# Second MoE: 104 columns for a slot's last chunk, and a stretch without choices behind slot 2

## The chip, the cores and the metric

The kernel runs on one core of a Trainium2 chip. The metric is the device time of one execution in microseconds (us). The kernel before took 532.64 us (median of three runs, 532.51 to 535.22).

## The reference, cut to what matters

Attention over two batches of 448 tokens feeds a first gated MoE layer (`a * b @ w_out`), and its 896 rows of 768 numbers feed the second MoE, which the change is about:

```python
def _moe2_ref(x, expert_emb, tau, w1, w2):        # x 896x768, 8 experts, w1 768x1024, w2 1024x768
    ...
    expert_idx = np.argmax(logits, axis=1)        # one expert a token
    ...
    for e in range(E):
        mask = expert_idx == e
        if not mask.any():
            continue
        h = np.maximum(x[mask] @ w1[e], 0.0)
        out[mask] = gate_w[mask, None] * (h @ w2[e])
```

How many tokens an expert gets is known only on the chip. On the inputs of these runs the counts are, in falling order, 329, 227, 203, 77, 44, 16, 0 and 0 (the reference's own choice of experts gives them).

## The kernel before, in words

**Stages.** Attention and the first MoE take until 367 us. Beside the first MoE's last product (L897), `choose`, `places` and `tables` route the tokens: they count them, sort the experts by their counts into eight *slots*, the largest first, and write a table of row numbers for each slot. `places` also writes one number `many` (L797 to L800: the larger of slot 3's count less 64 and slot 4's count), which `count_many` puts into a register of every engine; `counts` does that with each slot's count.

**A slot and its chunks.** A slot's tokens are taken in chunks of 128 (called windows, `w`). One chunk is this work:
- `gather` (POOL) fetches the token rows by an indirect DMA, `turn2` (PE, L1081) transposes them, and ACT copies them to `xt`.
- `first` (L1088) makes the hidden rows: 144 products on PE (L1099 to L1101). The weights of the expert are the stationary operand (128 columns loaded), and the chunk's `n` tokens are the columns that move. ACT writes the relu twice (L1107, L1108), POOL the low half (L1109).
- `second` (L1135): 48 products (L1151), the hidden rows of the tokens stationary, 256 or 512 columns of the second weights moving; ACT scales the result (L1155), and POOL scatters it to the output (`scatter`, L1115).

`whole(j)` is a slot's first chunk, always of 128 columns, and `more(j, w)` are its others: behind a condition `cv[j] > w * P` (L1192) stand the chunk and, nested in it, the condition for the next one. From slot 4 on, a slot with at most 64 tokens goes through `part` instead, with 64 columns (`first` with n = 64, `second_small` L1128). For slot 4 `many` decides between the two (the condition labelled `s4`, L1261): where it is at most 64, `chain` runs the rest as parts, each behind a condition on its count (`c4_5`, L1255).

**Choices.** A condition is a compare and branch that each engine which takes part in it executes in its own order of instructions. `more`'s conditions are taken by PE, ACT and POOL; those of `s4`, the chain and the late slots also by DVE and SP. `hint` and `hint_slot` (L1173, L1179) tell the engines of a condition's outcome ahead of it. At the end of a nested condition each engine runs a wait for its own outstanding work before it goes on.

**The weights.** SP issues the loads of an expert (L864, L866; 14 pieces) into four raw buffers, DVE splits each piece into a high and a low half (L877, L881) in one of three buffers, `bufA`, `bufB`, `bufC` in turn. `load_expert(j + 2)` stands ahead of slot j's work; from expert 5 on it is behind a condition of its own on DVE and SP (L1168). So expert 5 is loaded while slots 2, 3 and 4 run, into the buffer that slot 2 uses.

**The order now.** With the counts above PE runs slot 0 with three chunks, slots 1 and 2 with two each, slot 3 with one, all of 128 columns; then slots 4 and 5 as parts of 64. The order of instructions in this stage is that of the code; the first MoE's planner has no part in it.

Of the kernel before, what the change touches and what calls it, by code (L numbers as in the profile page):

```python
# [12 lines left out]
F32 = mybir.dt.float32  # L13
I32 = mybir.dt.int32
# [3 lines left out]
ALU = mybir.AluOpType  # L18
# [67 lines left out]
def fused_kernel(ctx: ExitStack, tc: tile.TileContext, q, k, v, w_a, w_b, w_out, emb, tau, w1, w2, out):  # L86
    nc = tc.nc
    B, NPR, _, S = q.shape
# [12 lines left out]
    SQ = -1.0 / math.sqrt(D)  # L101

    NLOAD, FEW = 5, 4
    NFIRST, NC1 = 4, 8
    RK = dict(S=(-2.0, 5.0, -1.0), M=-1.2, T=-8.1, H=-6.8, L=0.0, V=2.7, sq=5.4, X=-9.5, C1A=10, C1B=13.0)
    NRAW2 = 4
# [660 lines left out]
    def places():  # L767
# [25 lines left out]
        nc.vector.tensor_reduce(meta[:, 1, :], tmp, axis=AX.X, op=ALU.add)  # L793
        metai = cst.tile([1, 2, E], I32, name="metai")
        nc.vector.tensor_copy(metai, meta[0:1])
        mny = cst.tile([1, 1], F32, name="mny")
        nc.vector.scalar_tensor_tensor(mny, meta[0:1, 1, FEW - 1 : FEW], -P / 2.0, meta[0:1, 1, FEW : FEW + 1], op0=ALU.add, op1=ALU.max)  # L797
        nc.vector.tensor_scalar(mny, mny, 0.0, None, op0=ALU.max)
        mnyi = cst.tile([1, 1], I32, name="mnyi")
        nc.vector.tensor_copy(mnyi, mny)  # L800
        R["many"] = mnyi

# [174 lines left out]
            skip_runtime_bounds_check_because="only compared with constants")[1]  # L977

    def count_many():
        cv["many"] = nc.values_load_multi_w_load_instructions(  # L980
            R["many"], engines=ALL, min_val=0, max_val=NT,
            skip_runtime_bounds_check_because="only compared with a constant")[1][0]

    for j in range(0, E, 2):
        at(G2(3, 2 + 2 * j), 9, lambda j=j: counts(j))
# [81 lines left out]
    def gather(j, w):  # L1067
        io = bass.IndirectOffsetOnAxis(ap=gidi[:, j * NW + w : j * NW + w + 1], axis=0)
        nc.gpsimd.indirect_dma_start(xr_(j, w), None, xs, io)  # L1069

    def turn2(j, w):
        xt = xt_(j, w)
        xr = xr_(j, w).bitcast(F16)
        if w == 0:
            pt = ps.tile([P, 2048], F16, tag="big1", name=f"ptx{j}_{w}", bufs=1)
            halves = [pt[:, :DM], pt[:, DM : 2 * DM]]
        else:
            halves = [ps.tile([P, 1024], F16, tag=g, name=f"ptx{j}_{w}{g}", bufs=1)[:, :DM] for g in ("sm", "held")]
        for l, pt_ in enumerate(halves):
            for kc in range(KC):  # L1080
                nc.tensor.transpose(pt_[:, kc * P : (kc + 1) * P], xr[:, (l * KC + kc) * P : (l * KC + kc + 1) * P], id16)  # L1081
        if w == 0:
            nc.scalar.activation(xt.rearrange("p k t -> p (k t)"), pt[:, : 2 * DM], AF.Copy)
        else:
            for l in range(2):
                nc.scalar.activation(xt[:, l * KC : (l + 1) * KC, :].rearrange("p k t -> p (k t)"), halves[l], AF.Copy)
# [48 lines left out]
    def second(j, w, n, mid=()):  # L1135
        u = f"{j}_{w}_{n}"
        hth, htl = hs[min(w, 1)]
        _, _, w2h, w2l = expert(j)
        py = big(f"py{u}", min(w, 1))
        parts = (slice(512, DM), slice(0, 512))  # L1140
        halves = (range(FC // 2), range(FC // 2, FC))
        for k, (a, fs, p) in enumerate([(hth, fs, p) for fs in halves for p in range(2)] + [(htl, range(FC), p) for p in range(2)]):
            if k == 3:
                for fn in mid:
                    fn()
                if w == 0 and j + 1 > FEW:
                    hint_slot(j + 1)
            ns = parts[p]
            for f in fs:
                for w_ in (w2h, w2l) if a is hth else (w2h,):  # L1150
                    nc.tensor.matmul(py[:, ns], a[:, f, :], w_[:, f, ns], start=k < 2 and f == 0 and w_ is w2h,  # L1151
                                     stop=a is htl and f == FC - 1)
        y = m2y.tile([P, DM], F32, tag="y", name=f"y{u}", bufs=1)
        for ns in parts:
            nc.scalar.activation(y[:n, ns], py[:n, ns], AF.Copy, scale=scl[:n, j * NW + w : j * NW + w + 1])  # L1155
        scatter(j, w, n, y)
# [13 lines left out]

    def hint(j, w):
        if w < nwin[j]:
            tc.mark_branch_hint_location(f"w{j}_{w}", hint=cv[j] > w * P, engines=EN)  # L1173

    def hint_slot(j):
        if NLOAD <= j < E:
            tc.mark_branch_hint_location(f"w{j}_0", hint=cv[j] > 0, engines=ALL)
        elif j == FEW:
            tc.mark_branch_hint_location(f"s{j}", hint=cv["many"] > P // 2, engines=ALL)  # L1179

    def ahead(j, w):

        return j < NEXT1 if w == 1 else j < 2 and w == 2

    def next_turns(j, w):
        return [lambda: turn2(j, w + 1)] if w + 1 < nwin[j] and ahead(j, w + 1) else []

    def more(j, w):

        if w == nwin[j]:  # L1190
            return
        with tc.If(cv[j] > w * P, preferred_fallthrough_block=True, label=f"w{j}_{w}"):  # L1192
            hint(j, w + 1)
            if not ahead(j, w):
                gather(j, w)
                turn2(j, w)
            first(j, w, P)
            second(j, w, P, next_turns(j, w))
            more(j, w + 1)

    NEXT1 = 3

# [11 lines left out]
        nc.scalar.activation(raw[:1, :1], xt_(0, 1)[:1, 0, :1], AF.Copy)  # L1214
        return raw

    def whole(j):
        mid = next_turns(j, 0)
        if j == 0:
            first(0, 0, P, lambda: (hint(0, 1), gather(0, 1), gather(1, 0)))  # L1220
            gather(0, 2)
            gates()
            windows()
            scaled()
            mid += [lambda: load_expert(2, True)]
        else:
            if j >= FEW:
                hint(j, 1)
            if j + 1 == FEW:
                hint_slot(FEW)  # L1230
            first(j, 0, P, lambda: hint(j, 1) if j + 1 < FEW else None)
            gathers(j)
        if j >= FEW:
            more(j, 1)
        if j + 1 < E:
            mid += [lambda: turn2(j + 1, 0)]
        if j == 0:
            mid += [scales, lambda: gathers(0)]
        second(j, 0, P, mid)
        if j + 1 < FEW:  # L1240
            more(j, 1)

    def part(j):
# [14 lines left out]
                chain(i, j + 1)  # L1258

    def slot(j):  # L1260
        with tc.If(cv["many" if j == FEW else j] > P // 2, preferred_fallthrough_block=True, label=f"s{j}") as many:  # L1261
            if j == FEW:
                more(j - 1, 1)
                load_expert(j + 2)
            whole(j)
            slots(j + 1)
        with many.Else():
            if j == FEW:
                load_expert(j + 2)
            chain(j, j)  # L1270

    def slots(j):
        if j == E:
            return
        if j < FEW:
            if 0 < j < E - 2:
                load_expert(j + 2)
            whole(j)
            slots(j + 1)
        elif j < NLOAD:  # L1280
            slot(j)
        else:
            with tc.If(cv[j] > 0, preferred_fallthrough_block=True, label=f"w{j}_0"):
                if j < E - 2:
                    load_expert(j + 2)
                slot(j)
# [43 lines left out]
```

## Time and profile before

| | |
|---|---|
| median of three runs | 532.64 us |
| the profiled execution | 532.47 us, of which the span of its instructions is 530.8 us |
| PE busy in the span | 508.7 us, 96% |
| DVE, ACT, POOL busy | 402.9, 212.0, 118.6 us |
| second MoE's chunks (from the end of L897 to PE's last product) | 367.2 to about 524 us |
| from there to the end of the span | 7 us |

An execution's own time is a little longer than the span of its instructions (1.7 us here). In the rows below, times are microseconds from the start of the span. PE is TensorE's matmul part, PEld its loads of the stationary operand, PEq (PEldq) its sequencer, where branches and waits run; DVE, ACT, POOL and SP are the other engines. In a row of the timeline the first number is the start, the second the duration, the brackets the idle time of that engine just before with what ended it. A matmul's duration reaches from its start to the end of its results, so that the durations of neighbours overlap: how long one takes in a row of many is read from start to start.

### The profile page before, as it was taken

What the parts mean: (1) busy time and instruction counts of PE and PEld (TensorE: products, weight loads), DVE (VectorE), ACT (ScalarE), POOL (GpSimd) and SP (SyncE); (2) the same over time, 40 slices, a digit from 0 to 9 for tenths busy, and PEclk for the clock granted to TensorE, in tenths of its full rate; (3) what the DMA queues carried; (4) which work ended last, traced back from release to release, by engine and by line L of the source; (5) the groups of instructions that cost most, each with busy time, mean ns of one, the idle gap of its engine ahead of it and who ended that gap; (6) DMA issues with size and microseconds to landing.
All of it is one profiled execution on the core that took longest, in us unless ns stands there. A gap on an engine that the chain in (4) does not pass through costs nothing. (4 is left out here: it accounts for less than half of the span.)

```text
span 530.8 us, 12641 instructions
## 1 busy us (share of the span) xinstructions
PE 508.7 (96%) x5121; PEld 343.4 (65%) x5121; DVE 402.9 (76%) x643; ACT 212.0 (40%) x492; POOL 118.6 (22%) x123
## 2 busy tenths in 40 slices
PE   6999799999999999999999999999999999999994
PEld 3777477765555555545547666667788778876883
DVE  3899589999999966899712579984589497694970
ACT  3888998896233222343310111113422133231232
POOL 7877445110000000000000000000532242233333
PEclk9999799999999999999999999999999999999998
DMA  7853313036356533789720189991597479584761
GB/s 221 280 165 92 127 53 114 7 116 127 130 192 207 190 111 119 198 195 268 190 40 3 61 308 291 315 315 50 153 325 250 136 229 325 181 250 181 217 201 48
DMA packets 44793, 92.63 MB, mean 175 GB/s; under 512 B 22118, under 2 KB 25190, under 8 KB 44720
## 3 DMA queue, kind: packets, MB, share of 16 engines
q1 hardware_dynamic: 42816, 83.77, 50.7%
q0 software_dynamic: 1904, 7.90, 4.8%
q8 instruction: 45, 0.74, 0.6%
q14 instruction: 28, 0.23, 0.1%
HBM read 79.46 MB, written 8.26 MB: 165 GB/s over the span
## 5 line engine op out<-in xcount | busy, mean ns | idle before, releaser
L502 PE MATMUL ab<-bufA 128*128 128x448 f16 x864 | 167.7, 352 | 0.0
L502 PEld LDWEIGHTS <-bufA 128*128 128x128 f16 x864 | 83.3, 98 | 74.7
L897 PE MATMUL x<-woc,gL 128*128 128x512 f16 x336 | 56.5, 326 | 0.0
L392 ACT ACTIVATE pr<-sc,mn 112x336 f32<-112x336 f32 (+2 forms) x96 | 46.6, 499 | 12.3 <-DVE mn L376 12.3
L1003 POOL DMA_INDIRECT x<-xse,gidi x1 | 1.3, 1277 | 222.7 <-DMA rw<-in_moe_w_dram 222.7
L897 PEld LDWEIGHTS <-gL 128*128 128x128 f16 x336 | 32.4, 98 | 21.0
L376 DVE TENSOR_REDUCE mn<-sc 112x2 f32<-112x896 f32 (+3 forms) x48 | 33.9, 726 | 8.4 <-PE sc L365 8.2
L1109 POOL TENSOR_TENSOR hl<-hr,hh 128x512 f16<-128x512 f32 (+1 forms) x20 | 26.4, 1320 | 61.0 <-ACT hr L1108 56.2
L359 PE MATMUL sc<-ld,ld 64*112 64x448 f32 (+3 forms) x192 | 35.7, 473 | 4.0 <-DMA ld<-in_q_dram 4.0
L407 DVE TENSOR_TENSOR tbuf<-pt,tbuf 112x448 f16<-112x448 f32 x60 | 35.9, 612 | 4.3 <-ACT tbuf L404 4.0
L401 PE MATMUL pt<-id,pr 112*112 112x112 f32 x240 | 34.8, 272 | 4.1 <-ACT pr L392 2.6
L260 DVE SCALAR_TENSOR_TENSOR cv<-raw,cv 128x768 uint32<-128x768 uint32 x36 | 34.4, 955 | 0.9
L404 ACT ACTIVATE tbuf<-pt 112x448 f16<-112x448 f32 x60 | 32.6, 550 | 5.9 <-PE pt L401 5.6
L264 DVE SCALAR_TENSOR_TENSOR cv<-raw,cv 128x768 uint32<-128x768 uint32 x36 | 34.4, 954 | 0.4
L881 DVE SCALAR_TENSOR_TENSOR bufC<-rw,bufC 128x768 f16<-128x768 f32 (+1 forms) x28 | 33.2, 1185 | 1.4
L1151 PEld LDWEIGHTS <-hh 128*128 128x128 f16 x256 | 24.4, 98 | 14.6
L510 DVE TENSOR_TENSOR asb<-asb,ab 128x448 f32<-128x448 f32 x24 | 14.8, 618 | 24.7 <-PE ab L502 24.5
L1107 ACT ACTIVATE hh<-ph 128x512 f16<-128x512 f32 (+1 forms) x20 | 11.1, 554 | 54.4 <-PE ph L1101 54.4
L881 DVE SCALAR_TENSOR_TENSOR bufA<-rw,bufA 128x768 f16<-128x768 f32 (+1 forms) x28 | 30.0, 1073 | 1.4
L881 DVE SCALAR_TENSOR_TENSOR bufB<-rw,bufB 128x768 f16<-128x768 f32 (+1 forms) x28 | 30.0, 1072 | 1.4
L903 ACT ACTIVATE row<-x 128x768 f16<-128x768 f32 x7 | 5.7, 810 | 63.3 <-PE x L897 54.4
L877 DVE TENSOR_SCALAR bufC<-rw 128x768 f16<-128x768 f32 (+1 forms) x28 | 19.3, 688 | 13.4 <-PEq L1192 7.4
(243 smaller groups left out, 1199.4 us busy)
## 6 DMA issues: line engine op xcount, KB each, us to landing
rw<-in_moe_w_dram SPq DMA_DIRECT2D x36, 512.0 KB, 4.8
rw<-in_moe_w_dram SPq DMA_DIRECT2D x48, 384.0 KB, 3.9
raw<-in_moe_w_a_dram SPq DMA_DIRECT2D x12, 768.0 KB, 6.0
raw<-in_moe_w_b_dram SPq DMA_DIRECT2D x12, 768.0 KB, 7.6
raw<-in_moe_w_out_dram SPq DMA_DIRECT2D x12, 768.0 KB, 4.3
ld<-in_k_dram SPq DMA_DIRECT2D x12, 224.0 KB, 4.6
ld<-in_q_dram SPq DMA_DIRECT2D x12, 224.0 KB, 2.7
ld<-in_v_dram SPq DMA_DIRECT2D x12, 224.0 KB, 4.5
```

The source lines that it names most:

```text
L260: nc.vector.scalar_tensor_tensor(t, r()[:, :, 1], 0xC0000000, t, op0=ALU.bitwise_and, op1=ALU.bitwise_or)
L264: nc.vector.scalar_tensor_tensor(t, r()[:, :, 0], 29, t, op0=ALU.logical_shift_right, op1=ALU.bitwise_or)
L359: nc.tensor.matmul(sc[:CP, j, o : o + W], qt[hd, c * CP : W], kt[hd, :W], start=n == 0, stop=False)
L376: nc.vector.tensor_reduce(mns[pi][:, c, :], sc[:CP, :, o : o + W], axis=AX.X, op=ALU.min)
L392: nc.scalar.activation(pr[:, d : d + W], sc[:CP, jj, o : o + W], AF.Exp, bias=mn[:, c, jj : jj + 1], scale=-1.0, accum_out=sums[pi][:, c, ...
L401: nc.tensor.transpose(pt[:CP, cs], prs[g][:, cs], id32[:CP, :CP])
L404: nc.scalar.activation(tbufs[g % NTB][:, 0, :S], pts[g][:CP, :S], AF.Copy)
L407: nc.vector.tensor_tensor(tbufs[g % NTB][:, 1, :S], pts.pop(g)[:CP, :S], tbufs[g % NTB][:, 0, :S], op=ALU.subtract)
L502: nc.tensor.matmul(gt[i][:, :S], w[:, h, i, kc, :], x[:, kc, ts], start=kc == n == 0, stop=kc == KC - 1 and n == 2)
L881: nc.vector.scalar_tensor_tensor(dl, R.pop(("raw", j, pc))[:, :n], SE, dh, op0=ALU.mult, op1=ALU.subtract)
L897: nc.tensor.matmul(xp[:, ns], G(f)[:, a, tk], woc[:, f, l, ns], start=st, stop=sp)
L1109: nc.gpsimd.tensor_tensor(lv, hr, hv, op=ALU.subtract)
```

## The change

- A new constant TAIL = 104. A chunk after the first with more than 104 tokens runs with 128 columns as before (`chunk(j, w, P)`); the condition of `more` is now `cv[j] > w * P + TAIL`. It has an else branch, `tail(j, w)`: behind a condition of its own without a label or a hint stands the same chunk with 104 columns.
- In `second` the stationary operand and the output are cut to the chunk's n tokens, `a[:, f, :n]` and `py[:n]`.
- `places` writes two numbers, `s` (the old `many`) and `light`: the largest of slot 3's count less 40, slot 4's count, and slot 2's count less 168.
- Behind slot 2's first chunk stands a new condition `light`, taken by all five engines, with its hint in slot 2's `whole`. Where `light` is over 64, the code goes on as before. Else: slot 2's tail, the load of expert 5 (under its own condition), slot 3 with 104 columns, the load of expert 6 (likewise), then the chain of parts from slot 4. Slot 3's condition for a second chunk and the condition `s4` don't stand on that way.

With the counts of these inputs `light` is max(77 - 40, 44, 203 - 168) = 44, so the else way is taken. The tails are slot 0's third chunk (329 - 256 = 73 tokens, at most 104), slot 1's second (99) and slot 2's second (75); slot 3 (77) is whole with 104 columns.

```diff
--- before.py
+++ after.py
@@ -101,6 +101,7 @@
     SQ = -1.0 / math.sqrt(D)
 
     NLOAD, FEW = 5, 4
+    TAIL = 104
     NFIRST, NC1 = 4, 8
     RK = dict(S=(-2.0, 5.0, -1.0), M=-1.2, T=-8.1, H=-6.8, L=0.0, V=2.7, sq=5.4, X=-9.5, C1A=10, C1B=13.0)
     NRAW2 = 4
@@ -793,10 +794,13 @@
         nc.vector.tensor_reduce(meta[:, 1, :], tmp, axis=AX.X, op=ALU.add)
         metai = cst.tile([1, 2, E], I32, name="metai")
         nc.vector.tensor_copy(metai, meta[0:1])
-        mny = cst.tile([1, 1], F32, name="mny")
-        nc.vector.scalar_tensor_tensor(mny, meta[0:1, 1, FEW - 1 : FEW], -P / 2.0, meta[0:1, 1, FEW : FEW + 1], op0=ALU.add, op1=ALU.max)
-        nc.vector.tensor_scalar(mny, mny, 0.0, None, op0=ALU.max)
-        mnyi = cst.tile([1, 1], I32, name="mnyi")
+        mny = cst.tile([1, 2], F32, name="mny")
+        at_ = lambda j: meta[0:1, 1, j : j + 1]
+        nc.vector.tensor_scalar(mny[:, :1], at_(FEW - 1), -P / 2.0, 0.0, op0=ALU.add, op1=ALU.max)
+        nc.vector.tensor_scalar(mny[:, 1:], at_(FEW - 1), float(P // 2 - TAIL), 0.0, op0=ALU.add, op1=ALU.max)
+        nc.vector.tensor_tensor(mny, mny, at_(FEW).to_broadcast([1, 2]), op=ALU.max)
+        nc.vector.scalar_tensor_tensor(mny[:, 1:], at_(FEW - 2), float(P // 2 - P - TAIL), mny[:, 1:], op0=ALU.add, op1=ALU.max)
+        mnyi = cst.tile([1, 2], I32, name="mnyi")
         nc.vector.tensor_copy(mnyi, mny)
         R["many"] = mnyi
 
@@ -977,9 +981,9 @@
             skip_runtime_bounds_check_because="only compared with constants")[1]
 
     def count_many():
-        cv["many"] = nc.values_load_multi_w_load_instructions(
+        cv["s"], cv["light"] = nc.values_load_multi_w_load_instructions(
             R["many"], engines=ALL, min_val=0, max_val=NT,
-            skip_runtime_bounds_check_because="only compared with a constant")[1][0]
+            skip_runtime_bounds_check_because="only compared with a constant")[1]
 
     for j in range(0, E, 2):
         at(G2(3, 2 + 2 * j), 9, lambda j=j: counts(j))
@@ -1148,7 +1152,7 @@
             ns = parts[p]
             for f in fs:
                 for w_ in (w2h, w2l) if a is hth else (w2h,):
-                    nc.tensor.matmul(py[:, ns], a[:, f, :], w_[:, f, ns], start=k < 2 and f == 0 and w_ is w2h,
+                    nc.tensor.matmul(py[:n, ns], a[:, f, :n], w_[:, f, ns], start=k < 2 and f == 0 and w_ is w2h,
                                      stop=a is htl and f == FC - 1)
         y = m2y.tile([P, DM], F32, tag="y", name=f"y{u}", bufs=1)
         for ns in parts:
@@ -1170,13 +1174,13 @@
 
     def hint(j, w):
         if w < nwin[j]:
-            tc.mark_branch_hint_location(f"w{j}_{w}", hint=cv[j] > w * P, engines=EN)
+            tc.mark_branch_hint_location(f"w{j}_{w}", hint=cv[j] > w * P + TAIL, engines=EN)
 
     def hint_slot(j):
         if NLOAD <= j < E:
             tc.mark_branch_hint_location(f"w{j}_0", hint=cv[j] > 0, engines=ALL)
         elif j == FEW:
-            tc.mark_branch_hint_location(f"s{j}", hint=cv["many"] > P // 2, engines=ALL)
+            tc.mark_branch_hint_location(f"s{j}", hint=cv["s"] > P // 2, engines=ALL)
 
     def ahead(j, w):
 
@@ -1189,14 +1193,23 @@
 
         if w == nwin[j]:
             return
-        with tc.If(cv[j] > w * P, preferred_fallthrough_block=True, label=f"w{j}_{w}"):
+        with tc.If(cv[j] > w * P + TAIL, preferred_fallthrough_block=True, label=f"w{j}_{w}") as full:
             hint(j, w + 1)
-            if not ahead(j, w):
-                gather(j, w)
-                turn2(j, w)
-            first(j, w, P)
-            second(j, w, P, next_turns(j, w))
+            chunk(j, w, P, next_turns(j, w))
             more(j, w + 1)
+        with full.Else():
+            tail(j, w)
+
+    def chunk(j, w, n, mid=()):
+        if not ahead(j, w):
+            gather(j, w)
+            turn2(j, w)
+        first(j, w, n)
+        second(j, w, n, mid)
+
+    def tail(j, w):
+        with tc.If(cv[j] > w * P, preferred_fallthrough_block=True):
+            chunk(j, w, TAIL)
 
     NEXT1 = 3
 
@@ -1214,7 +1227,7 @@
         nc.scalar.activation(raw[:1, :1], xt_(0, 1)[:1, 0, :1], AF.Copy)
         return raw
 
-    def whole(j):
+    def whole(j, n=P):
         mid = next_turns(j, 0)
         if j == 0:
             first(0, 0, P, lambda: (hint(0, 1), gather(0, 1), gather(1, 0)))
@@ -1226,9 +1239,11 @@
         else:
             if j >= FEW:
                 hint(j, 1)
-            if j + 1 == FEW:
+            elif j == FEW - 1 and n == P:
                 hint_slot(FEW)
-            first(j, 0, P, lambda: hint(j, 1) if j + 1 < FEW else None)
+            elif j == FEW - 2:
+                tc.mark_branch_hint_location("light", hint=cv["light"] > P // 2, engines=ALL)
+            first(j, 0, n, lambda: hint(j, 1) if j < FEW - 2 else None)
             gathers(j)
         if j >= FEW:
             more(j, 1)
@@ -1236,8 +1251,8 @@
             mid += [lambda: turn2(j + 1, 0)]
         if j == 0:
             mid += [scales, lambda: gathers(0)]
-        second(j, 0, P, mid)
-        if j + 1 < FEW:
+        second(j, 0, n, mid)
+        if j < FEW - 2:
             more(j, 1)
 
     def part(j):
@@ -1258,7 +1273,7 @@
                 chain(i, j + 1)
 
     def slot(j):
-        with tc.If(cv["many" if j == FEW else j] > P // 2, preferred_fallthrough_block=True, label=f"s{j}") as many:
+        with tc.If(cv["s" if j == FEW else j] > P // 2, preferred_fallthrough_block=True, label=f"s{j}") as many:
             if j == FEW:
                 more(j - 1, 1)
                 load_expert(j + 2)
@@ -1272,9 +1287,24 @@
     def slots(j):
         if j == E:
             return
-        if j < FEW:
+        if j < FEW - 1:
             if 0 < j < E - 2:
                 load_expert(j + 2)
+            whole(j)
+            if j < FEW - 2:
+                slots(j + 1)
+                return
+            with tc.If(cv["light"] > P // 2, preferred_fallthrough_block=True, label="light") as many:
+                more(j, 1)
+                slots(j + 1)
+            with many.Else():
+                tail(j, 1)
+                load_expert(j + 3)
+                whole(j + 1, TAIL)
+                load_expert(j + 4)
+                chain("l", j + 2)
+        elif j == FEW - 1:
+            load_expert(j + 2)
             whole(j)
             slots(j + 1)
         elif j < NLOAD:
```

## Rows read from the trace of the kernel before

**Rows 1.** The page, parts 1 and 5: PE's busy time, and POOL's low halves.

```profile
PE 508.7 (96%) x5121; PEld 343.4 (65%) x5121; DVE 402.9 (76%) x643; ACT 212.0 (40%) x492; POOL 118.6 (22%) x123
...
L1109 POOL TENSOR_TENSOR hl<-hr,hh 128x512 f16<-128x512 f32 (+1 forms) x20 | 26.4, 1320 | 61.0 <-ACT hr L1108 56.2
```

**Rows 2.** Two stretches: busy us (count) of PE, PEld, DVE, ACT, POOL; PEclk; DMA.

```profile
280.00:367.20 87.20, 87.20 (x728) 54.87 (x726) 61.55 (x123) 12.53 (x22) 1.28 (x1) 1.00 0.59 200
524.00:531.00 7.00, 0.00 (x0) 0.00 (x0) 0.62 (x1) 0.57 (x1) 1.48 (x2) 0.72 0.23 68
```

**Rows 3.** PE's waits from 367 us on: us in total, times, longest; sequencer's events.

```profile
PE ph L1099 <- PEq L1192: 1.5, 3, 0.6
...
PE pyl L1128 <- POOL hl L1109: 0.2, 1, 0.2
...
L1192 PEldq EVENT_SEMAPHORE  x3: 51/51/51, 420.5 to 488.5; - x3
```

**Rows 4.** Timeline of PE: slot 3's first products with 128 columns, first and behind last.

```profile
489.07 0.22 PE L1099 MATMUL ph<-xt,bufA 128*128 128x128 f16 x1 [0.64 <-PEq L1192]
...
497.12 3.64 PE L1151 MATMUL py<-bufA,hh 128*128 128x256 f16 x24
```

**Rows 5.** Timeline of PE: slot 4's first products with 64 columns, likewise.

```profile
505.59 0.19 PE L1099 MATMUL ph<-xt,bufB 128*128 128x64 f16 x1
...
509.79 0.33 PE L1081 MATMUL ptx<-id,xr 128*128 128x128 f16 x3
```

**Rows 6.** Timeline of PE: second products of slots 2 and 3, last groups.

```profile
485.67 2.76 PE L1151 MATMUL py<-bufC,hl 128*128 128x256 f16 x16
...
500.59 0.83 PE L1081 MATMUL ptx<-id,xr 128*128 128x128 f16 x12
501.26 1.89 PE L1151 MATMUL py<-bufA,hh 128*128 128x512 f16 x8
502.99 2.76 PE L1151 MATMUL py<-bufA,hl 128*128 128x256 f16 x16
```

**Rows 7.** PEld's loads by form: count, busy us, mean ns, idle before.

```profile
L1151 PEld LDWEIGHTS <-hh 128*128 128x128 f16 x256 | 24.4, 98 | 14.6
...
L365 PEld LDWEIGHTS <-idb 112*112 112x112 bf16 x96 | 8.1, 136 | 14.5 <-issue 13.4
```

**Rows 8.** Timeline of PE in attention: four L365 products and the next line's.

```profile
40.95 0.41 PE L365 MATMUL sc<-maskb,idb 112*112 112x112 bf16 x4
41.19 0.19 PE L423 MATMUL po<-vh,tbuf 112*128 112x64 f16 x1
```

**Rows 9.** PEldq's compare-branches, count, ns min/median/max, first and last start.

```profile
L1192 PEldq COMPARE_BRANCH  x1: 475/475/475, 417.3 to 417.3; - x1
...
L1192 PEldq COMPARE_BRANCH  x1: 2940/2940/2940, 451.6 to 451.6; - x1
...
L1192 PEldq COMPARE_BRANCH  x1: 443/443/443, 485.3 to 485.3; - x1
...
L1261 PEldq COMPARE_BRANCH  x1: 342/342/342, 502.6 to 502.6; - x1
...
L1255 PEldq COMPARE_BRANCH  x3: 84/195/345, 512.7 to 524.2; - x3
```

**Rows 10.** Timelines and branches at slots 4 and 5: DVE, then SP, then PE.

```profile
488.56 0.69 DVE L877 TENSOR_SCALAR bufC<-rw 128x1024 f16<-128x1024 f32 x1 [7.37 <-PEq L1192]
...
514.61 0.96 DVE L881 SCALAR_TENSOR_TENSOR bufC<-rw,bufC 128x768 f16<-128x768 f32 x1
518.88 0.62 DVE L1132 TENSOR_SCALAR ys<-pyr,scl 64x384 f32<-64x384 f32 x1 [3.32 <-DVEq L1168]
...
L1261 SPq COMPARE_BRANCH  x1: 58/58/58, 508.7 to 508.7; - x1
...
L1168 SPq COMPARE_BRANCH  x1: 57/57/57, 514.0 to 514.0; - x1
...
519.55 0.35 PE L1128 MATMUL pyl<-bufC,hh 128*64 128x384 f16 x1
```

## The prediction

> **What bounds the kernel now.** I read the page's totals first: PE is busy for 508.7 of 530.8 us [rows 1]. The stretches say where that share is whole: from 280 us through the end of the first MoE PE is busy in every microsecond at a granted clock of 1.00, and in the last 7 us it does nothing [rows 2]. So until 524 us time is won only by taking work or pauses from PE; the last scatter behind it moves along with PE's end. Third, PE's own waits in the second MoE: three behind conditions, 1.5 us together, one for each event wait of its sequencer there, and at the end 0.2 us for POOL's low half [rows 3]. PE is the bound of this stage and nearly without gaps.
>
> Which code runs is the next question. From the token counts, before runs eight chunks of 128 and two parts of 64; POOL's low halves, two a chunk, come 20 times [rows 1], which is these ten. After it, slot 0's third chunk (73 tokens), slot 1's second (99), slot 2's second (75) and slot 3 (77) have 104 columns, and `light` is 44, so the way without choices is taken.
>
> **Term 1: narrower first products.** In slot 3 the 144 first products take 497.12 - 489.07 = 8.05 us, 55.9 ns each [rows 4]; in slot 4, with 64 columns, 509.79 - 505.59 = 4.20 us, 29.2 ns each [rows 5]. That is 26.7 ns for 64 columns, 0.417 ns a column; 24 columns less are 10.0 ns less, 104 columns 45.9 ns. Four chunks of 144 products at 10.0 ns: **-5.77 us**. A line through 64 and 128 is an estimate for 104; if the pitch were in proportion to the columns (55.9 x 104/128 = 45.4 ns) it would be -6.05. As the other bound, should 104 columns lie 1.2 ns above the line, as 64 lie above half of 128 (29.2 against 28.0), 8.8 ns are left, or -5.05. I take the line: its two ends are the same code.
>
> **The second products don't get shorter.** The tokens are the stationary operand there, and the 256 or 512 weight columns that move stay. Eight of 512 take 502.99 - 501.26 = 1.73 us, 216 ns each; slot 3's first 24 of them end at 500.59, 3.47 us after 497.12, so that with 1.73 us in eight of 512 the 16 of 256 take 1.74 us, 109 ns each [rows 4, 6]. What changes is the load: 104 columns in place of 128. A load of 128 columns is recorded with 98 ns, the nearest narrower one, 112 columns in attention, with 136 ns [rows 7]. A longer record need not cost time: four of those L365 products start within 41.19 - 40.95 = 0.24 us, 60 ns each with their loads [rows 8], and the shortest product that has to cover a load here takes 109 ns. I cost it at nothing. Bounds: nothing, and 136 ns uncovered for each of 4 x 48 = 192 loads, 26.1 us.
>
> "TensorE: Matmul & The Clock Gate" of the Trainium skill, section "Weight-path perf modes — Fast Weight Load (FWL) and DoubleRow", speaks against this change: a fast load is used only where exactly 128 weights are loaded and not in FP32, so 104 would lose it. The longer record of 112 agrees with it; by its section "LDWEIGHTS (loading the stationary operand)" a plain load of 104 columns is estimated at 104/1.2 = 87 ns, under 109, and the sum would be the same.
>
> **Term 2: slot 2's end without a join.** Today slot 2's last products start at 485.67 and last 2.76 us, to 488.43 [rows 6], and slot 3's first product starts at 489.07 after 0.64 us of idle for PE's sequencer [rows 4]. Where no join stands between (slot 3 to slot 4), the old group ends at 502.99 + 2.76 = 505.75 and the next product starts at 505.59 [rows 5, 6], 0.16 us before that. By the code the pause belongs to a condition that is not taken: the skipped side makes up the semaphore counts of the work left out, and PE's sequencer first waits there for PE's own products (the event at 488.5 is slot 2's [rows 3]). On the new way slot 2's tail stands in a condition that is taken, and none untaken lies between it and slot 3; the two sides of `light` are made even behind the chain. I take 0.64 + 0.16 = **-0.80 us**; bounds -0.80 and 0. The pauses behind slots 0 and 1, the rest of the 1.5 us, stay.
>
> **Term 3: the end.** DVE takes `s4` and the load conditions just ahead of the last part; it then stands 3.32 us and scales slot 4's half at 518.88 [rows 10], POOL's queue follows, and PE's last group waits 0.2 us for POOL [rows 3]. With the condition `s4` gone from this place: **-0.2 us**; bounds -0.2 and +0.3 (a new lateness of the same kind, a little over the old).
>
> **Term 4: a jump at slot 0's end.** Slot 0's second chunk (full, taken) now has an else behind it: a 104-column chunk of 144 and 48 products with a load each, 384 PE instructions, that PE must jump over behind its drain, with nothing queued to cover the jump. PE's far branches in this run last 475, 2940, 443, 342 and 345 ns, a near one 195 ns (the middle one of the chain's three) [rows 9]. Mean of the far ones less the near one: 0.91 - 0.20 = **+0.7 us**. Bounds: 0 and 2940 - 195 = 2.75 us. The mean, since one in five is the long kind and I can't tell which this is. The other new jumps (into slot 0's and slot 1's tails, into the else behind `light`) are hinted ahead, and PE takes them while up to 3 us of queued products run: `s4` was taken at 502.6, 3.0 us before the product behind it at 505.59 [rows 5, 9].
>
> **Work that moves or grows, at no cost.** `places` has one more small operation on one partition: it runs beside the first MoE's last products, where PE is full and DVE isn't [rows 2], as does each engine's read of one more register. ACT, POOL and the scatters handle fewer elements; PE waits for none but at the end. The new wait to look at is `light` on SP and DVE, in front of expert 5's load. SP stood from 508.7 to 514.0 behind `s4`, 5.3 us, and DVE 3.32 us [rows 10]; the same now falls ahead of the load. Cover: DVE idles 7.37 us for slot 2 to give its buffer back, until 488.56 [rows 10], and only a later first piece than that costs. What follows on SP are expert 5's 14 loads through four raw buffers, and on DVE all casts; then PE, which needs the expert at slot 5. The last cast ends 514.61 + 0.96 = 515.57, slot 5's second products start at 519.55 [rows 10]: 4.0 us of slack, of which PE's gain after slot 2 (slots 2 and 3, about 2.3 us) takes a part. I cost it at nothing; bounds 0 and 5.3 - (4.0 - 2.3) = 3.6 us.
>
> **Sum:** -5.77 - 0.80 - 0.2 + 0.7 = -6.07 us. The profiled execution took 532.47 us around a span of 530.8; so 526.4 us by its own time, and as it lies 0.17 us under the median of the runs, **526.6 us** against 532.64. A difference under 0.5% (2.7 us) can't be told from none here.
>
> **Rivals.**
> - *The jump at slot 0's end is of the long kind*, 2.75 in place of 0.7 us: 528.6 us. For it, one of five far branches was, and nothing is queued behind the drain; against it, four of five. Chance 0.18. "Runtime: NRT & Kernel Launch" of the Trainium skill, section "Instruction fetch mechanics", has a taken branch stall where its target is outside the two pages held; 384 instructions ahead may be in or out, and the trace's 2940 ns shows that stalls of this size occur.
> - *Expert 5 comes late* because `light` stands ahead of its load: 1 to 3.6 us, 527.6 to 530.2 us. Against it, the 7.37 us of idle. Chance 0.08.
> - *The stationary loads of 104 columns show.* For it, the record of 112 is 136 ns against 98. If that difference alone appears, 192 x 38 ns = 7.3 us, and the kernel is slower, at 533.9 us; a wholly uncovered load gives 552.7. It decides from 6.07 us/192 = 32 ns a load. Against it, the 60 ns starts in attention. Chance 0.05.
> - *The change doesn't do what it says*: a tail of more than 104, or `light` over 64. The counts speak against it, near ties between experts aside. 532.6 us, chance 0.04.
> - *More pauses go than I count*: PE's jump is hidden, and the joins behind slots 0 and 1 get shorter too, by up to 1.2 us: 524.6 to 525.9. Chance 0.09.
>
> **How the numbers follow.** The forecast itself has 0.56, 525.4 to 527.6: below, the lower bounds of terms 1 and 4 (0.28 and 0.7 us under the sum) and 0.2 us for the spread of runs; above, half of the upper bounds of terms 1 to 3 (0.72, 0.80 and 0.5). The range of 8 in 10 takes in the long jump and part of the late expert and of the shorter joins: 525.0 to 529.4. Faster by over 0.5% is under 530.0: the forecast, the long jump, nearly all of the late expert and the fewer pauses, 0.90. Slower by over 0.5% asks for loads that cost more than (6.07 + 2.7)/192 = 46 ns each: 0.03. The rest, 0.07, is the same.
>
> **What would show it.** First products of 104 columns in the four chunks at 46 ns from start to start; their second products at 109 and 216 ns as now (over that, the loads show). PE's waits: two behind conditions instead of three, and slot 0's either 0.6 or some 1.3 or over 3 us. Slot 3 starting without idle behind slot 2. DVE's first cast of expert 5 right when slot 2 ends. Wrong would be a pitch of 104 columns near 56 ns, or PE waiting for `bufC` at slot 5.

## The result and the profile after

The changed kernel takes 526.41 us (median of 6 runs, 524.57 to 529.84) against 532.88 us (6 runs, 530.84 to 535.22). The ratio is 0.9881, interval 0.984 to 0.9922: faster by 1.2%. The forecast was 526.6 us, its range 525.0 to 529.4.

The profiled execution took 525.34 us, its span is 523.55 us, 7.22 us under before's 530.77. To see where that comes from I cut both spans at two points, the start of slot 0's first product and that of PE's last. Ahead of the first, 1.32 us are gone (it starts at 365.89 instead of 367.21 us), which I don't count for the change: in the thirteen traces of this study this start lies anywhere from 365.80 to 368.82. Between the two, the stage, 156.46 us became 151.38 (-5.08). Behind it 7.10 became 6.28 (-0.82). So the change itself shows -5.90 us in this pair of traces.

The page, PE's row as in [rows 1]:

```profile
PE 500.7 (96%) x5109; PEld 340.2 (65%) x5109; DVE 403.1 (77%) x645; ACT 209.3 (40%) x490; POOL 115.2 (22%) x123
```

PE has 8.0 us less to do, 12 products fewer among them, and is still the bound. The timeline of PE at slot 3, as in [rows 4]:

```profile
482.02 2.11 PE L1155 MATMUL py<-bufC,hl 128*104 128x256 f16 x10
483.96 0.21 PE L1103 MATMUL ph<-xt,bufA 128*128 128x104 f16 x1
...
490.56 0.28 PE L1155 MATMUL py<-bufA,hh 128*104 128x256 f16 x1
```

The 144 first products of 104 columns take 490.56 - 483.96 = 6.60 us, 45.8 ns each; slot 3 begins without idle behind slot 2. The second products of slot 1's tail in the timeline, to be read beside [rows 6]:

```profile
444.58 5.37 PE L1155 MATMUL py<-bufB,hh 128*104 128x256 f16 x32
449.78 2.76 PE L1155 MATMUL py<-bufB,hl 128*104 128x256 f16 x16
452.38 0.22 PE L1103 MATMUL ph<-xt,bufC 128*128 128x128 f16 x1
```

All 48 take 452.38 - 444.58 = 7.80 us, which is 24 x 109 + 24 x 216 ns, as before. The loads under them are recorded longer, as [rows 7] made likely (columns as there, the same line's two forms):

```profile
L1155 PEld LDWEIGHTS <-hh 128*104 128x104 f16 x128 | 14.8, 127 | 5.0
L1155 PEld LDWEIGHTS <-hh 128*128 128x128 f16 x128 | 12.2, 98 | 7.3
```

127 ns against 98, and none of it in the time. PE's waits from 367 us on, as in [rows 3]:

```profile
PE ph L1103 <- ACT y L1159: 2.1, 1, 2.1
PE ph L1104 <- issue: 0.8, 1, 0.8
PE ts L1061 <- DVE pas L1054: 0.2, 1, 0.2
PE ptx L1085 <- issue: 0.2, 1, 0.2
```

No row names a condition any more, and the wait for POOL is gone. The two large ones are new. The timeline has their places:

```profile
419.78 0.23 PE L1103 MATMUL ph<-xt,bufB 128*128 128x128 f16 x1 [2.07 <-ACT y L1159]
...
438.48 0.21 PE L1103 MATMUL ph<-xtw,bufB 128*128 128x104 f16 x1
439.53 0.22 PE L1104 MATMUL ph<-xtw,bufB 128*128 128x104 f16 x1 [0.84 <-issue]
```

The first is slot 1's first product; ACT, which the row blames, is only what came last. The second lies inside slot 1's tail, behind its 34th product, where the program has nothing to wait for. PE's branches, as in [rows 9], explain the first:

```profile
L1211 PEldq COMPARE_BRANCH  x1: 5189/5189/5189, 414.5 to 414.5; - x1
...
L1211 PEldq COMPARE_BRANCH  x1: 190/190/190, 449.4 to 449.4; - x1
```

The jump at slot 0's end takes 5.19 us of the sequencer, the near one at slot 1's end 0.19. Below, a pause is the extra from one product's start to the next over the usual pitch (109, 216 ns), which is a little more than the idle in brackets: 2.24 and 1.00 us here; before's three are 0.61, 0.61 and 0.81 us.

| term (us) | forecast | measured |
|---|---|---|
| first products, 4 x (8.04 - 6.60) | -5.77 | -5.76 |
| second products | 0 | 0 |
| slot 2's end, pause 0.81 gone | -0.80 | -0.81 |
| the last part's wait for POOL | -0.2 | -0.33 |
| slot 0's end, pause 0.61 to 2.24 | +0.7 | +1.63 |
| slot 1's end, pause 0.61 gone | 0 | -0.61 |
| inside slot 1's tail, new pause | - | +1.00 |
| 12 transposes in slot 1's second chunk gone | - | -0.67 |
| parts' first products (4.20 to 4.47, 4.21 to 4.45) | - | +0.51 |
| POOL's joins behind PE's end | 0 | -0.82 |
| sum | -6.07 | -5.86 |

The unforeseen terms nearly cancel (+1.00 + 0.51 - 0.61 - 0.67 - 0.82 = -0.59, against 0.93 more at slot 0's end), so the total alone says little about the steps. POOL's joins: a join is the place behind a condition where an engine waits for its own work and makes up the semaphore counts of the side not run. Before, POOL did that twice behind the last scatter, at L1255 and L1261, now once:

```profile
L1270 POOLq INC_SWDGE_SEM  x1: 717/717/717, 519.5 to 519.5; - x1
```

The two of before lasted 732 and 699 ns, so the one that went is worth some 0.7 of the 0.82 us.

### The profile page after: what moved, and what is told of

The parts are those of the page before. It is cut to its first block, busy times and chain, and to the rows that moved or that the text cites. A ratio compares the mean times of both kernels' runs of the same rounds, so it can differ in the third digit from the quotient of the medians.

```text
span 523.5 us, 12581 instructions
## 1 busy us (share of the span) xinstructions
PE 500.7 (96%) x5109; PEld 340.2 (65%) x5109; DVE 403.1 (77%) x645; ACT 209.3 (40%) x490; POOL 115.2 (22%) x123
## 5 line engine op out<-in xcount | busy, mean ns | idle before, releaser
L1113 POOL TENSOR_TENSOR hl<-hr,hh 128x512 f16<-128x512 f32 (+2 forms) x20 | 24.8, 1240 | 62.3 <-ACT hr L1112 55.9
L1155 PEld LDWEIGHTS <-hh 128*128 128x128 f16 (+1 forms) x256 | 26.9, 112 | 12.3
L881 DVE TENSOR_SCALAR bufC<-rw 128x768 f16<-128x768 f32 (+1 forms) x28 | 22.7, 809 | 12.9 <-DMA rw<-in_moe_w_dram 5.6
L885 DVE SCALAR_TENSOR_TENSOR bufC<-rw,bufC 128x768 f16<-128x768 f32 (+1 forms) x28 | 31.3, 1118 | 1.4
L1111 ACT ACTIVATE hh<-ph 128x512 f16<-128x512 f32 (+2 forms) x20 | 10.4, 522 | 51.0 <-PE ph L1105 47.2
```

The lines of the kernel that those rows point to most:

```text
L885: nc.vector.scalar_tensor_tensor(dl, R.pop(("raw", j, pc))[:, :n], SE, dh, op0=ALU.mult, op1=ALU.subtract)
L1155: nc.tensor.matmul(py[:n, ns], a[:, f, :n], w_[:, f, ns], start=k < 2 and f == 0 and w_ is w2h, stop=a is htl and f == FC - 1)
```

## The experiments

The numbers given are the time's median and, from the trace, the stage as cut above (156.46 before, 151.38 changed). One part of the stage belongs to no edit here: slot 0's first chunk, from its first product to the second chunk's, takes 20.7 to 20.8 us in before, in the changed kernel's first trace and in three of the experiments (the one called "the same once more", the one without the else and moved, the way with choices kept), and 20.0 to 20.3 us in the eight other traces. It is in every difference between a trace of the one kind and one of the other.

**The columns alone.** The code of before with

```diff
-            first(j, w, P)
-            second(j, w, P, next_turns(j, w))
+            n = 104 if (j, w) in ((0, 2), (1, 1), (2, 1)) else P
+            first(j, w, n)
+            second(j, w, n, next_turns(j, w))
```

the same for slot 3 in `whole`, and `second` cut to `a[:, f, :n]`.

> The code of before, with 104 columns set by hand for the four chunks (slot 0's third, slots 1's and 2's second, slot 3), no new condition. Theory (the columns are a term of their own, 4 x 144 x 10.0 ns): first products of these chunks 46 ns from start to start, second products at 109 and 216 ns, the three pauses at slot ends as in before (0.61, 0.61, 0.81 us); the stage from slot 0's first product to PE's last goes from 156.5 to 150.7 us, the time down by 5.8 us. Rival (the narrower stationary loads show, or later waits take the gain back): second products above 109 or 216 ns, or new waits, and less than 4 us gained.

Measured: 527.12 us (ratio to before 0.9909, 0.9886 to 0.9931), stage 151.94, so -4.5 instead of -5.8, and 0.6 of the 4.5 lie in slot 0's first chunk. The products are as the theory had them (6.60 us in each of the four). What takes the rest back are waits, in PE's waits from 367 us:

```profile
PE ph L1099 <- PEq L1192: 2.0, 3, 0.9
PE pyr L1128 <- DVEq L1168: 1.0, 1, 1.0
```

The choice of `s4` on DVE, covered in before until POOL's 0.2 us, now holds the last part for 1.0 us (1.16 over the pitch), because PE comes to it 6.4 us earlier (513.11 for 519.55) and DVE ends its last cast only 5.3 us earlier (510.30 for 515.57). The three pauses are not all as in before either: 0.68, 1.05 and 0.80 us. The second goes with slot 1's branch, hinted like the others, which was the long one in before (2940 ns in [rows 9]) and takes more here:

```profile
L1192 PEldq COMPARE_BRANCH  x1: 3600/3600/3600, 447.6 to 447.6; - x1
```

The rival is right that later waits take a part back, and right with its 4 us (3.9 without slot 0's first chunk); the loads have none in it.

**The code alone.** In the changed kernel's `first` and `second`:

```diff
+        n = P if n == TAIL else n
```

> The changed code with its conditions and jumps, but its tails run with 128 columns. Theory (the code's own gains and losses about cancel: after slot 0 +1.6, in slot 1's tail +1.0, in the parts +0.5, against -0.6, -0.8, -0.7, -0.3 and -0.9 at the slot ends, the left-out transposes, the end wait and behind PE's end): the stage is 151.4 + 5.8 = 157.1 us, and the time within 1 us of before. Rival (the forecast's own view, the code without choices gains 0.8 + 0.2 and loses 0.7): the stage 0.3 us under before's 156.5 and no pause over 1.3 us behind slot 0.

Measured: 530.58 us (0.9974, 0.9951 to 0.9996), stage 155.60, 0.86 us under before. Neither number was met: the pause behind slot 0 is 0.86, not 2.24, the one in slot 1's tail 2.03, not 1.00, and the parts have none. The pauses of the new code aren't constants. Of the rival, the pause behind slot 0 (under 1.3 us) came true. Of the 0.86 us, 0.7 lie in slot 0's first chunk; in the rest of the stage the code by itself gives under 0.2 us, the pauses eating what the slot ends save, and behind PE's last product another 0.84 (6.26 for 7.10).

**The changed kernel once more**, unedited.

> The changed kernel as it is, once more: how far do its pauses repeat? Theory (the pauses are fetches of code over DMA, whose time varies): the pause behind slot 0 lies anywhere from 0.8 to 2.3 us (0.86, 1.79 and 2.24 in the three kernels that have this jump), the one in slot 1's tail from 0.8 to 2.1 us, and all products take the same 46, 56, 109 and 216 ns. Rival (fixed costs of these joins): 2.24 and 1.00 us to within 0.1.

Measured: one execution, 526.96 us, stage 151.87. The pauses are 0.80 and 2.39 us: the theory. Behind the second one, though, PE was slow. The stretches around it (columns as in [rows 2]):

```profile
434.00:437.80 3.80, 3.80 (x49) 2.79 (x46) 2.88 (x5) 1.06 (x3) 0.31 (x1) 1.00 0.93 332
437.80:440.20 2.40, 0.20 (x5) 0.05 (x2) 0.55 (x1) 0.00 (x0) 1.46 (x1) 0.97 0.99 376
440.20:443.50 3.30, 3.27 (x39) 3.28 (x40) 1.52 (x2) 0.00 (x0) 0.00 (x0) 0.50 1.01 401
443.50:446.70 3.20, 3.20 (x73) 3.20 (x71) 0.44 (x1) 0.93 (x2) 0.96 (x1) 1.00 0.57 207
```

After 2.4 us almost without products the granted clock is 0.50 for 3.3 us, the lower of its two levels, 1.2 GHz; the 110 products behind the pause take 6.57 us instead of 5.05. That is 1.5 us more for this pause than the pause itself.

**No else at slot 0's second chunk.**

```diff
-        with tc.If(cv[j] > w * P + TAIL, ..., label=f"w{j}_{w}") as full:
+        with tc.If(cv[j] > bound(j, w), ..., label=f"w{j}_{w}") as full:
...
-        with full.Else():
-            tail(j, w)
+        if bound(j, w) > w * P:
+            with full.Else():
+                tail(j, w)
...
+    def bound(j, w):
+        return w * P + (TAIL if (j, w) != (0, 1) else 0)
```

The hint uses the same bound. A second chunk of slot 0 then always has 128 columns, whatever its count.

> The changed kernel, but slot 0's second chunk has no else: its condition is cv > 128 again, with 128 columns, so that nothing has to be jumped over at slot 0's end. Theory (the 2.24 us behind slot 0 are the unhinted jump over that else, whose code has to be fetched): the pause goes to under 0.1 us, and the time falls by 2.2 us against the changed kernel, to about 524.2. Rival 1 (a join's wait for PE's own products comes in its place, as in before): 0.6 us stay, 524.8. Rival 2 (the pause belongs to the end of slot 0, whatever stands there): 2.2 us stay, 526.4. The pause inside slot 1's tail may move with the code.

Measured: 522.46 us (0.9823, 0.9797 to 0.9849), stage 147.22. The branch and PE's waits:

```profile
L1215 PEldq COMPARE_BRANCH  x1: 186/186/186, 414.9 to 414.9; - x1
```

```profile
PE ptx L1085 <- DMA xr<-xs,gidi: 0.2, 1, 0.2
```

The jump is a near one, the pause is gone, neither rival came. The stage fell by 4.2 us, more than the 2.24: the pause in slot 1's tail is 0.17 us now and those of the parts are gone in this trace (0.8 and 0.5 us), and 0.6 us lie in slot 0's first chunk. The next run of the same kernel has the parts' pauses and the longer first chunk again, so these are not of this edit.

**The same once more.**

> The kernel without the else of slot 0's second chunk, as it is, once more beside the two others. Theory: the pause behind slot 0 stays under 0.1 us and the one in slot 1's tail under 0.5 us, PE's granted clock at 1.00 through both; the time 522.5 us, 4 us under the changed kernel. Rival (a lucky run, pauses vary from run to run as in the changed kernel): pauses of 1 us and more, 524 us or over.

Measured: 523.51 us (0.9815, 0.9789 to 0.9842), stage 148.13. No pause behind slot 0 or in slot 1's tail; the parts have 0.26 and 0.25 us again. So this kernel is 1.8% faster than before, and it repeats; the intervals of both ratios (up to 0.9849) lie nearly wholly under the changed kernel's (from 0.984).

**A short else there.** Only for slot 0's second chunk the tail becomes

```diff
+            if (j, w) == (0, 1):
+                second(j, w, TAIL)
```

> The changed kernel, with the else of slot 0's second chunk (not taken here) cut to its 48 second products, so the jump over it is 96 PE instructions and not 384. What the cut leaves out of the computation isn't run with these counts. Theory (the jump costs what its target's fetch costs, and a near target is at hand): the branch takes about 0.2 us, as near ones do, and the pause behind slot 0 is under 0.1 us. Rival (any jump over an else, or the join behind it, costs it): the branch again 3.8 to 5.2 us, the pause 0.8 to 2.3 us.

Measured: one execution, 524.12 us, stage 147.32; the branch:

```profile
L1211 PEldq COMPARE_BRANCH  x1: 292/292/292, 416.7 to 416.7; - x1
```

No pause behind slot 0; slot 1's tail has one of 0.43 us. The join with its else is there and costs no pause; the distance of the target does.

**Slot 1's tail moved by 120 PE instructions.** In slot 1's second chunk of 128, not run here:

```diff
-            chunk(j, w, P, next_turns(j, w))
+            chunk(j, w, P, next_turns(j, w) + ([lambda: turn2(1, 2)] * SH if (j, w) == (1, 1) else []))
```

with SH = 5.

> The changed kernel, with five more transposes' worth of code (120 PE instructions) in the branch of slot 1's second chunk that is not taken, so that slot 1's tail lies 120 instructions further on in the code. Theory (the 1.00 us pause after 34 products of slot 1's tail is PE's instruction fetch, which depends on where the jump lands): no pause there, or one after another number of products; the stage down to about 150.4 us. Rival (the products wait there for data or a semaphore): the same pause of 1.0 us after 34 products.

Measured: one execution, 523.30 us, stage 148.88. No pause in slot 1's tail; its first products take 6.60 us. Nothing but the place of the code differs there, so the pause is PE's instructions coming late. The jump at slot 0's end is as far as ever, its pause 1.79:

```profile
L1212 PEldq COMPARE_BRANCH  x1: 4744/4744/4744, 414.5 to 414.5; - x1
```

**Without the else, and moved by 216 instructions** (nine of these transposes).

> The kernel without the else of slot 0's second chunk, with 216 more PE instructions in the branch of slot 1's second chunk that is not taken, so that more code of the tail's landing line is left. Theory (fetch): the remaining pause of 0.17 us in slot 1's tail goes, no pause of PE over 0.1 us from slot 0's third chunk to slot 4; the time as without the shift, 522.3 us, within the runs' spread. Rival: the pause stays at 0.17 us or grows to the 1.0 to 2.4 us of the changed kernel, where the clock can fall.

Measured: 524.23 us (0.9849, 0.9817 to 0.9881), stage 149.26. Slot 1's tail has no pause, but slot 2's tail, moved by the same shift, has one of 1.07 us behind its 15th product:

```profile
PE ph L1103 <- issue: 0.9, 1, 0.9
```

The expectation of no pause up to slot 4 fell: shifting code mends one landing and spoils the next.

**The way with choices kept.** On the kernel without that else:

```diff
-            with tc.If(cv["light"] > P // 2, ..., label="light") as many:
+            with tc.If(cv["light"] > -1, ..., label="light") as many:
```

and its hint likewise.

> The kernel without the else of slot 0's second chunk, with light's condition made true always (light > -1): the way with choices behind slot 2, so slot 3 has 128 columns again and s4 stands ahead of slot 4; the tails of slots 0 to 2 keep 104. Theory (the code without choices is worth what it removes: slot 3's 24 columns 1.44 us, s4 on DVE ahead of the last part 0.3 to 1.5 us, one more join of 0.8 us on POOL behind PE's end): 2.5 to 3.8 us over the kernel without that else, about 525 to 526 us, with PE's last part waiting for DVE or POOL again. Rival (only the columns count): 1.4 us over it, 523.9.

Measured: 529.03 us (0.9937, 0.9907 to 0.9968), 5.5 to 6.6 us over the two medians without the else; stage 151.64, 3.5 to 4.4 us over. Slot 3's columns are in it (1.44) and, outside the stage, POOL's join behind PE's end (7.06 instead of 6.2 us). DVE and POOL are not waited for, so that part of the theory failed. The rows are DVE's last cast and its scaling in front of the last part, for [rows 10]:

```profile
501.97 0.96 DVE L885 SCALAR_TENSOR_TENSOR bufC<-rw,bufC 128x768 f16<-128x768 f32 x1
511.22 0.62 DVE L1136 TENSOR_SCALAR ys<-pyr,scl 64x384 f32<-64x384 f32 x1 [8.28 <-PE pyr L1132]
```

DVE's casts end at 502.93, 12.6 us earlier than before's (515.57); it takes `s4` at 502.4 and then waits for PE, not PE for it. In the place of that wait stands a jump into slot 2's tail, which has no hint on this way:

```profile
L1199 PEldq COMPARE_BRANCH  x1: 4847/4847/4847, 465.8 to 465.8; - x1
```

It costs a pause of 2.11 us; with slot 3's 1.44 that is the 3.5 us of stage over the second run without the else. So the worth of the way without choices depends on what hints the other way has.

**112 columns** (TAIL = 112).

> The changed kernel with 112 columns in place of 104; the same way through the code with these counts. Theory (the pitch lies on the line of 0.417 ns a column through 64 and 128): 49.2 ns from start to start in the four chunks, 4 x 144 x 3.3 ns = 1.9 us more in first products; second products at 109 and 216 ns. Rival (steps of the pitch, for one of 32 columns): 46 ns as with 104, or 56 as with 128.

Measured: one execution, 529.26 us, stage 153.85. Slot 0's third chunk in PE's timeline:

```profile
404.14 0.21 PE L1103 MATMUL ph<-xtw,bufA 128*128 128x112 f16 x1
...
411.22 0.28 PE L1155 MATMUL py<-bufA,hh 128*112 128x256 f16 x1
```

7.08 us, 49.2 ns each: the line holds. Against the changed kernel's second trace, whose pauses are the same (0.80 and 2.42 us, and again a fall of the clock), the stage is 1.98 us longer; 1.9 was expected.

**Before without slot 1's transposes for a chunk that doesn't come.**

```diff
-        return j < NEXT1 if w == 1 else j < 2 and w == 2
+        return j < NEXT1 if w == 1 else j < 1 and w == 2
```

and slot 1's gather for it left to that chunk.

> The kernel before without the 12 transposes (and the gather) that slot 1's second chunk makes ahead for a third chunk that doesn't come. Theory (they are work of PE that the changed kernel leaves out with its tail, a gain that the forecast did not count): 12 x 56 ns = 0.67 us less from slot 1's second chunk to slot 2, the stage from 156.5 to 155.8 us. Rival (the transposes fill a gap): no change there beyond 0.2 us.

Measured: one execution, 530.58 us, stage 155.19. From the second products of slot 1's second chunk on, in PE's timeline:

```profile
444.98 5.36 PE L1151 MATMUL py<-bufB,hh 128*128 128x256 f16 x32
450.18 2.76 PE L1151 MATMUL py<-bufB,hl 128*128 128x256 f16 x16
453.38 0.23 PE L1099 MATMUL ph<-xt,bufC 128*128 128x128 f16 x1 [0.44 <-PEq L1192]
```

453.38 - 444.98 = 8.40 us, against 9.08 in before: 0.68 us. The theory; the other half microsecond of the stage is not from this: slot 0's first chunk is 0.67 us shorter, and the rest is a little longer.

## Why the prediction was right, and which steps were not

*Term 1* was right to 0.01 us, and so was its line through 64 and 128, with 112 as a further point (49.2 ns, the line gives 49.2).

*The second products* cost nothing more, as taken. The record of a 104-column load is 127 ns against 98 for 128 columns, and the products above it keep 109 and 216 ns. "TensorE: Matmul & The Clock Gate" in the Trainium skill ("Weight-path perf modes — Fast Weight Load (FWL) and DoubleRow") says that a fast load needs 128 weights; the longer record agrees with it, and no run here shows a loss from it. The rival built on these loads falls.

*Term 2* was right for slot 2 and stopped one slot short. Its reason, that the pause belongs to a condition not taken, holds for slot 1's tail too, which stands in a taken condition now: 0.61 us more than the step allowed by which the pauses behind slots 0 and 1 stay. So the wait at the end of a nested condition, told above of every condition, comes only with one that is not taken.

*Term 3* was right in place and nearly in size (0.33 for 0.2), but its reason, that `s4` is gone, is not the one shown. With narrow columns in the code of before, `s4` on DVE holds PE for 1.16 us and POOL for 0.37; with the way with choices kept, `s4` is there too and PE waits for neither, as DVE's casts end 12.6 us earlier. The earlier casts (see expert 5) are enough by themselves.

*Term 4* named the right jump, and the wrong price and cover. Its price is the mean of five jumps that all have a hint in the code, of which one was long; this exit has none, and took 3.75 to 5.19 us of the sequencer in all five traces that have it. The step that failed is "behind its drain, with nothing queued to cover the jump". The sequencer is at the jump at 414.53, while the last queued product starts at 417.32; the jump takes 5.19 us. What is exposed is a pause of 0.80 to 2.24 us over five traces with this jump, where the 0.61 of before is saved: +0.2 to +1.6 in place of +0.7. That the cause is the target's fetch is shown: the same exit with a near target (186 and 292 ns) has no pause, else or not, and in the first of these two traces no packet of the instruction queue runs from the jump at 414.95 to slot 1's first product, where the far jump has one (last section). "Instruction fetch mechanics" in "Runtime: NRT & Kernel Launch" of the Trainium skill says that a jump out of the held pages stalls for a fetch; these traces agree.

*The other new jumps*, "hinted ahead" and taken "while up to 3 us of queued products run": that was true of the jump and false of what follows. The jump into slot 1's tail takes 0.36 us, hidden; but 34 products behind its landing the next piece of code comes late: 1.00, 2.03, 2.39 and 2.42 us in the four traces with this place of the code, none to 0.43 elsewhere. In these four a packet of the instruction queue starts at 437.24, 437.82, 437.75 and 438.65 us, and PE goes on 2.3 to 2.5 us after it each time. The forecast had no term for it.

*The end*: that "the last scatter behind it moves along with PE's end" missed POOL's join for `s4`, within 0.82 us; and the change list missed the 12 transposes, 0.67, that slot 1's tail doesn't make.

*Expert 5* was late by no means. The forecast expected its first cast at slot 2's end and less slack. The rows, to be read beside [rows 10]: DVE's first and last cast, PE's second products of slot 5.

```profile
476.58 0.69 DVE L881 TENSOR_SCALAR bufC<-rw 128x1024 f16<-128x1024 f32 x1 [5.50 <-PE ph L1105]
...
504.29 0.96 DVE L885 SCALAR_TENSOR_TENSOR bufC<-rw,bufC 128x768 f16<-128x768 f32 x1
...
513.50 0.35 PE L1132 MATMUL pyl<-bufC,hh 128*64 128x384 f16 x1
```

The cast starts 7.4 us ahead of slot 2's end (483.96), when the last first product there has read the buffer, and the slack is 513.50 - 505.25 = 8.25 us, not 4.0. Where no untaken condition stands behind the chunk, DVE waits for the products that read a buffer and not for the join. So `light` on SP and DVE cost PE nothing.

So the total was right by luck, by cancelling: two costs of about 1 us and one of 0.5 were missed, and three gains of 0.6 to 0.8 us.

Open: why the pauses of one kernel change from run to run and why the one behind slot 0 is short where the one in slot 1's tail is long (0.86 and 2.03, 0.80 and 2.39 and 2.42, against 2.24 and 1.00). The traces say only that a late start of the fetch makes the pause long; what sets the start wasn't tried. Open too is what holds the parts' first products for 0.25 us each in some traces. The changed code has these in the traces in which slot 0's first chunk is long, the changed kernel's first and three from one other chip, and in none of the six from two further chips, so they may be no cost of the change.

## What to carry to other kernels

Narrower moving columns gained what their pitch said on a bound PE, and narrower stationary ones nothing; price them from two widths of the same loop. An else that the common way has to jump over is not free where the jump is far: here leaving out the one else that slot 0 jumps was worth some 3 us more, and a shorter else took the pause away too; a hint for this jump was not tried. Where a change shortens the bound engine, count again what the other engines do in front of its last wait, and all the work that the new branch leaves out.

## What the runs showed of the hardware that was not expected

A far jump's fetch does not start with the jump. In the changed kernel's trace the DMA queues carry weights alone from 414.5 to 417.3 us; the one packet of the instruction queue is in the stretch behind it:

```profile
q8 instruction: 1, 0.02, 5.2%
```

It starts at 417.36, 2.8 us after the jump, and the branch ends 2.4 us later, at 419.72. In the second trace of the same kernel these are 1.4 us (415.28 to 416.67) and 2.4 us (to 419.03). Over the five traces with this jump the fetch starts 1.0 to 2.8 us after it, and the branch ends 2.3 to 2.8 us later. The products queued in front of the jump, some 3 us, thus hid the time until the fetch started and little else in the first trace, and 1.6 of the fetch's 2.4 us in the second.

And a pause can cost more than itself: two of 2.39 and 2.42 us inside slot 1's tail were followed by 3.3 us at half the granted clock, 1.5 us more in the first of them, while one of 2.24 us behind slot 0 was not.
